# Gate and value of three token chunks in seven products of 64x64 tiles, with the last batch's attention and the weight sums moved ahead of them

## The chip, the core and the metric

The kernel runs on one core of a Trainium2 chip. The metric is the time of one execution on the device in microseconds; the kernel before takes 289.92 us, the median of three runs (289.42 to 290.87). Everything is float32. The engines are named as the profile names them: PE is TensorE's matrix multiply and PEld its weight loads, DVE is VectorE, ACT is ScalarE, POOL is GpSimd, SP is the engine that issues most DMAs. PSUM holds what PE writes, in eight banks of 128 partitions by 512 numbers; SBUF holds everything else.

## What is computed

A polynomial sketch attention over four batches, four heads, 1088 positions of 32 numbers each, and then a gated feed-forward layer over all 4 x 1088 = 4352 tokens of 128 numbers:

```python
# attention, for each batch and head
a, b = S1 @ x, S2 @ x                        # 8 numbers each
phi(x) = outer(a, b)                         # 64 features
kv, z = phi(k).T @ v, phi(k).sum(over positions)
x = (phi(q) @ kv) / (phi(q) @ z + 1e-6)
# then, over x as (4352, 128), with 1536 hidden units
gate = 1 / (1 + exp(-(x @ w_gate)))
val = x @ w_val
out = (gate * val) @ w_out
```

## The kernel before

The four batches of attention write their result, transposed, into one SBUF tile `xT` of 128 partitions (one for each input feature) by 4352 tokens. The feed-forward layer takes the tokens in chunks of 512: chunks 0 to 7, and chunk 8 of 256 tokens. A chunk needs the batches that its tokens lie in: chunk 5 ends in batch 2, chunk 6 takes 192 tokens of batch 2 and begins batch 3, chunk 7 and 8 lie in batch 3.

**A wave** (`w1`, line 556) computes the gate and the value of 128 hidden units for a chunk: four matmuls with all 128 rows of the array, two for each of gate and value, because each is split in two column halves of 64 hidden units (`128*64` in the profile; the two halves run side by side). A float32 matmul is two instructions. ACT takes the sigmoid of the gate (line 564), DVE multiplies it with the value (line 599, for chunk 8 line 592), and the result `g` goes to SBUF. Twelve waves make a chunk; chunk 8 takes two times 128 units in a wave and has six. The PSUM tile of a wave has two banks and there are two such tiles, so wave n+2 can start when DVE has done the product of wave n. Waves are counted from 0; chunk 5 begins with wave 60, chunk 8 with wave 96.

**The output** of chunks 1 to 7 is already computed by a scheme with seven products instead of eight, of pairs of waves (`w2_a`, `w2_b`, line 381). It splits the tokens, the hidden units and the output features in halves; POOL makes the four sums of `g` that it needs (`token_sums`, line 371), the sums of the weights stand ready in `ws`. Each product has 256 columns and is `128*64`. At the end of a chunk ACT and DVE put the result together (lines 486 to 533) and SP stores it (line 393). Chunk 8's output is computed with plain products (`w2_end`, line 451), and its end is the end of the kernel (`store_end`, line 407).

**The order of the work** on PE, DVE, ACT and POOL is that of the program text; nothing reorders it. `slot(group, waves)` puts out one wave after another: it first puts out the DVE product of the wave before, then the output products that are due (`todo`), then the wave. The attention of batches 2 and 3 is set between the waves by a list of wave numbers, `plan`: transposing k and q (lines 662, 673), `begin` (the sketch, and DMAs that spread it through DRAM, line 864), the outer products (line 772), the sums of the features (line 946), `kv_all` (line 912), the products of q's features (line 892), and `parts`, which divides and writes `xT` (lines 1041 to 1304). For batch 3 the list is 48, 49, 52, 54, 57, 58, 59, 60, 62, 63, 65, 67. The k and q of batch 3 are loaded right after the last step but one of batch 2, at wave 41.

Of the kernel before, what the change touches and what calls it, by code (L numbers as in the profile page):

```python
# [8 lines left out]
F32 = mybir.dt.float32  # L9
# [3 lines left out]
ALU = mybir.AluOpType  # L13
ACTF = mybir.ActivationFunctionType
MUL = ALU.mult

P = 128


@with_exitstack  # L20
def kernel(
# [20 lines left out]
    assert DM == H * D == P and D == 32 and R == 8 and S % 32 == 0 and NTOK % 512 == 256  # L42

    T = S // 32

    NJK = 9
    KBASE = [0, 9, 17, 25]
# [5 lines left out]
    ld = ctx.enter_context(tc.tile_pool(name="ld", bufs=1))  # L53
    sbA = ctx.enter_context(tc.tile_pool(name="sbA", bufs=2))
    raw = ctx.enter_context(tc.tile_pool(name="raw", bufs=NJ // 2))
    sbN = ctx.enter_context(tc.tile_pool(name="sbN", bufs=1))
    sbG = ctx.enter_context(tc.tile_pool(name="sbG", bufs=3))

    dram = ctx.enter_context(tc.tile_pool(name="dram", bufs=1, space=bass.MemoryType.DRAM))

    psm = ctx.enter_context(tc.tile_pool(name="psm", bufs=2, space=bass.MemoryType.PSUM))
    pso = ctx.enter_context(tc.tile_pool(name="pso", bufs=1, space=bass.MemoryType.PSUM))
    ps2 = ctx.enter_context(tc.tile_pool(name="ps2", bufs=1, space=bass.MemoryType.PSUM))

    ctx.enter_context(tc.manual_schedule(
            engines={
# [62 lines left out]
    class Short:  # L129
# [31 lines left out]
        def total(self):  # L161
            nc.gpsimd.tensor_tensor(  # L162
                out=self.head, in0=self.head, in1=self.tail.bitcast(I32), op=ALU.add
            )
# [183 lines left out]

    xT = const.tile([P, NTOK], F32, tag="xT")

    moe = {"sum": -1, "ci": 0, "w": 0, "n": 0, "ready": 0, "acc": None, "gate": None, "todo": [], "late": [], "copies": []}

    def fast(ci):
        return 0 < ci < len(tok_chk) - 1 and tok_chk[ci][1] == TCH

    def weight_sums(n0, n1):
        w = w_sb[:, 2].rearrange("p (n f) d -> p f n d", f=2)[:, :, n0:n1]
# [22 lines left out]
    def product(out, lhsT, rhs, start, stop):  # L380
        nc.tensor.matmul(  # L381
            out=out, lhsT=lhsT, rhs=rhs, start=start, stop=stop, skip_group_check=True
        )
# [18 lines left out]

    def store_end(acc):
        b, r = divmod(tok_chk[-1][0], S)
        o_sb = [sbA.tile([P, P], F32, tag="o_sb", name="o_end") for _ in range(2)]
        for u, copy in enumerate((nc.scalar.copy, nc.vector.tensor_copy)):
            copy(out=o_sb[u], in_=acc[u])
        for u, eng in enumerate((nc.scalar, nc.sync)):
            eng.dma_start(
                out=bass.AP(  # L410
                    tensor=out.tensor,
                    offset=out.offset + (b * S + r // 32 + u) * DM,
                    ap=[[T * DM, 32], [2 * DM, 4], [1, DM]],
                ),
                in_=o_sb[u],
            )

    def w2(ci, j0, jn, g):
# [13 lines left out]
        if j0 + jn == NJ:  # L432
# [2 lines left out]
            moe["store"] = lambda: store(  # L435
                ci, lambda g4: o_sb[32 * g4 : 32 * g4 + 32], nc.scalar
            )

    def w2_end(ci, j0, jn, g):
        if j0 == 0:  # L440
            moe["sum"] = ci
            moe["acc"] = [
                pso.tile([P, TCH], F32, tag="acc0", name="moeout0")[:, :DM],
                ps2.tile([P, 2, TCH], F32, tag="two", name="moeout1")[:, 0, :DM],
            ]
        acc = moe["acc"]
        for u in range(2):
            for jj in range(jn):
                j = j0 + jj
                for c in (u * P, u * P + 64):  # L450
                    nc.tensor.matmul(  # L451
                        out=acc[u][c % P : c % P + 64],
                        lhsT=g[:, jj, c : c + 64],
                        rhs=w_sb[:, 2, j, :],
                        start=(j == 0),
                        stop=(j == NJ - 1),
                    )
        if j0 + jn == NJ:
            store_end(acc)


    fst = {}

# [31 lines left out]
    def add(out, in0, in1):  # L495
        nc.vector.tensor_tensor(out=out, in0=in0, in1=in1, op=ALU.add)  # L496
# [44 lines left out]
    def w1():  # L541

        ci = moe["ci"]
        t0, tw = tok_chk[ci]
        jn = TCH // tw
        j0 = moe["w"] * jn
        wv = psm.tile([P, 2, TCH], F32, tag="wave", name="wave")

        tp = tw // 2 if ci == 0 and j0 == 0 else tw
        turn = (moe["w"] // 2) % 2  # L550
        for o in range(0, tw, tp):
            for which in range(2):
                for jj in range(jn):
                    for c in (0,) if ci == 0 else (1 - turn, turn):
                        d = slice(0, P) if ci == 0 else slice(64 * c, 64 * c + 64)
                        nc.tensor.matmul(  # L556
                            out=wv[d, which, jj * tw + o : jj * tw + o + tp],
                            lhsT=w_sb[:, which, j0 + jj, d],
                            rhs=xT[:, t0 + o : t0 + o + tp],
                            start=True,  # L560
                            stop=True,
                        )
        sg = sbG.tile([P, TCH], F32, tag="sg", name="sg")
        nc.scalar.activation(out=sg, in_=wv[:, 0], func=ACTF.Sigmoid)  # L564
        if ci == 0:
            if j0 == 0:
                step("final", 2)
                step("sign", 3, bank="acc1")
            if j0 == 1:
                step("final", 3)  # L570
            if 1 < j0 < NJ - 1:
                narrow_w(j0 + 1, 3)
            if j0 > 0:
                narrow_w(j0 + 2, 1)
                narrow_w(j0 + 2, 2)
            if j0 < 3:
                narrow_w(j0 + 3, 0)
            if j0 > 1:
                narrow_w(j0 + 4, 0)
            if j0 == NJ - 3:  # L580
                weight_sums(0, NJ // 4)
            if j0 == NJ - 1:
                weight_sums(NJ // 4, NJ // 2)
        if moe["w"] % 2 == 0:
            moe["g"] = sbG.tile([P, 2, TCH], F32, tag="g", name="g")
        pair, odd, n = moe["g"], moe["w"] % 2, moe["n"]

        def glu():
            g = pair[:, odd]
            todo = moe["todo"]  # L590
            if jn == 2:
                nc.vector.tensor_tensor(  # L592
                    out=g.rearrange("p (j u s y) -> p j y u s", j=2, u=2, y=4),
                    in0=wv[:, 1].rearrange("p (j y u s) -> p j y u s", j=2, u=2, y=4),
                    in1=sg.rearrange("p (j y u s) -> p j y u s", j=2, u=2, y=4),
                    op=MUL,
                )
            else:
                nc.vector.tensor_tensor(out=g, in0=wv[:, 1], in1=sg, op=MUL)  # L599
            if not fast(ci):  # L600
                lag = 4 if ci else 2
                part = (ci, j0, jn, g.rearrange("p (j t) -> p j t", j=jn))
                todo.append((n + lag, lambda: (w2_end if ci else w2)(*part)))
                return
            if not odd:
                moe["t"] = raw.tile([P, 4, HALF], F32, tag="w_in", name="tsum")
            token_sums(pair, moe["t"], odd)
            if odd:
                part = (ci, j0 // 2, pair, moe["t"])
                todo.append((n + 3, lambda: w2_a(*part)))  # L610
                todo.append((n + 4, lambda: w2_b(*part)))

        moe["gate"] = glu
        moe["w"] += 1
        moe["n"] += 1
        if j0 + jn == NJ:
            moe["ci"] += 1
            moe["w"] = 0
# [6 lines left out]
    def slot(group, waves, behind=None):  # L625

        if group is not None:
            group()
        todo = moe["todo"]
        for _ in range(waves):  # L630
            more = moe["ci"] < len(tok_chk)
            if more and sum(tok_chk[moe["ci"]]) > moe["ready"]:
                break
            glu()
            for _ in range(2 if moe["ci"] >= len(tok_chk) - 1 else 1):
                if moe["late"]:
                    moe["late"].pop(0)()
            while todo and todo[0][0] <= moe["n"]:
                todo.pop(0)[1]()
            if behind is not None:  # L640
                behind()
                behind = None
            if more:
                w1()
            for copy in moe["copies"]:
                copy()
            moe["copies"] = []
            if more:
                continue
            if not todo:  # L650
                break
            else:
                todo.pop(0)[1]()

    kT_of, qT_of = {}, {}

# [688 lines left out]
    slot(None, 1)  # L1345
    slot(lambda: parts(1), 1)
    moe["store"]()

    def until(n):
        slot(None, n - moe["n"])  # L1350

    plan = {2: (27, 29, 30, 31, 32, 34, 36, 37, 38, 39, 41, 43)}
    plan[3] = (48, 49, 52, 54, 57, 58, 59, 60, 62, 63, 65, 67)
    for b in range(2, B):
        at = iter(plan[b])
        until(next(at))
# [22 lines left out]
        load_kq(b + 1)  # L1379
        until(next(at))  # L1380
        slot(lambda: parts(b), 1)
    slot(None, 10**3)


# [28 lines left out]
```

## Time and profile before

| what | us |
| --- | --- |
| median of three runs | 289.92 |
| the profiled execution, span from its first to its last instruction | 288.1 |
| PE busy | 282.6 |
| DVE busy | 170.5 |
| POOL busy | 160.0 |
| ACT busy | 106.6 |
| start of wave 60 (first of chunk 5) in the chain that ended last | 174.26 |
| start of chunk 8's first wave there | 266.68 |
| end of the last matmul | 284.9 |

The span is one execution, taken by the profiler on the core; the 1.8 us between it and the median lie before its first and after its last instruction, or are the difference of one execution from another. In the profile's groups of instructions a row gives the source line, the engine, the operation, the tile written and those read, the shapes and the count, and behind the bar the busy time in us and the mean duration of one in ns. In the timeline a row begins with its start and its length in us; rows of equal instructions that follow each other are merged into one. A matmul's length there is longer than its share of PE, because matmuls are pipelined: the time from one start to the next is what it costs.

### The profile page before, as it was taken

The page shows a single profiled execution, that of the slowest core. Times are in us where ns is not written, and L with a number is a line of the kernel's source. Part 1 is how long each engine was busy: PE and PEld are TensorE (multiplying, and loading weights), DVE is VectorE, ACT ScalarE, POOL GpSimd, SP SyncE. Part 2 cuts the span into 40 slices and gives each one's busy share as a digit, 9 for nine tenths or more (in the row PEclk, how much of TensorE's full clock was granted, in tenths as well). Part 3 has the DMA queues.
Part 4 walks back from the last instruction along what each step waited for, and adds up shares of the span by engine and source line. Part 5 has one row for each costly group of instructions (what it writes and reads, how often), then busy time and mean ns, then how long its engine had stood idle before and what let it go on. Part 6 is the DMA issues. An engine that isn't in the chain of part 4 may idle for free.

```text
span 288.1 us, 5783 instructions
## 1 busy us (share of the span) xinstructions
PE 282.6 (98%) x2260; PEld 135.1 (47%) x2260; DVE 170.5 (59%) x292; ACT 106.6 (37%) x215; POOL 160.0 (56%) x222
## 2 busy tenths in 40 slices
PE   8899999999999999999999999999999999999995
PEld 4454433354444444535444445444444444444685
DVE  6977788945748547668446485767245223522571
ACT  3688833222334322523244222532243224421341
POOL 2666682667466387383565496483564646555200
PEclk9999999999999999999999999999999999999999
DMA  7995441766500385352000683020001000020012
GB/s 220 348 360 124 104 156 43 171 150 157 164 3 2 77 198 166 92 161 32 1 0 12 162 158 123 2 30 9 0 3 23 14 2 0 4 35 1 0 19 40
DMA packets 28891, 24.24 MB, mean 84 GB/s; under 512 B 18560, under 2 KB 24064, under 8 KB 28864
## 3 DMA queue, kind: packets, MB, share of 16 engines
q1 hardware_dynamic: 25888, 22.10, 30.1%
q10 hardware_dynamic: 2976, 1.77, 2.1%
q8 instruction: 18, 0.29, 0.4%
q14 instruction: 9, 0.07, 0.1%
HBM read 20.60 MB, written 3.26 MB: 83 GB/s over the span
## 4 chain that ended last, share of the span: by engine, by line
PE 97%; ACT 1%; POOL 0%; DVE 0%; issue 0%
PE wave L556 61%; PE prod L381 22%; PE moeout L425 4%; PE moeout L451 2%; PE warm L301 2%; PE kvz L912 1%; PE nps L1270 1%; PE kps L693 1%; PE kvz L899 1%; PE cqps L839 1%; PE nps L1102 0%; PE denj L1041 0%; PE nps L1054 0%; PE dps L1083 0%; ACT asb L810 0%; POOL gh L727 0%
## 5 line engine op out<-in xcount | busy, mean ns | idle before, releaser
L556 PE MATMUL wave<-xT,w_sb 128*64 128x512 f32 (+3 forms) x820 | 201.4, 565 | 0.1
L564 ACT ACTIVATE sg<-wave 128x512 f32<-128x512 f32 x102 | 60.9, 597 | 158.3 <-PE wave L556 152.3
L599 DVE TENSOR_TENSOR g<-wave,sg 128x512 f32<-128x512 f32 x96 | 66.1, 688 | 87.9 <-ACT sg L564 86.3
L371 POOL TENSOR_TENSOR tsum<-g,tsum 128x256 f32<-128x256 f32 x84 | 68.6, 817 | 71.0 <-DVE g L599 70.9
L556 PEld LDWEIGHTS wave<-xT,w_sb 128*64 128x64 f32 (+1 forms) x820 | 71.0, 140 | 72.7 <-issue 53.0
L371 POOL TENSOR_TENSOR tsum<-g 128x256 f32<-128x256 f32 x84 | 66.6, 793 | 22.1 <-DVE g L599 21.5
L381 PE MATMUL prod<-tsum,ws 128*64 128x256 f32 x252 | 68.4, 380 | 0.0
L381 PE MATMUL prod<-g,w_sb 128*64 128x256 f32 (+1 forms) x170 | 50.3, 378 | 0.0
L381 PEld LDWEIGHTS prod<-tsum,ws 128*64 128x64 f32 x252 | 34.0, 137 | 13.1 <-issue 9.7
L381 PEld LDWEIGHTS prod<-g,w_sb 128*64 128x64 f32 x170 | 23.0, 137 | 30.1 <-issue 25.8
L381 PE MATMUL prod<-tsum,w_sb 128*64 128x256 f32 x84 | 25.0, 380 | 0.0
L381 PE MATMUL prod<-g,ws 128*64 128x256 f32 x84 | 25.0, 379 | 0.0
L162 POOL TENSOR_TENSOR head<-head,tail 128x384 int32<-128x384 int32 (+1 forms) x13 | 13.2, 1023 | 4.4 <-DVE head L157 4.4
L381 PEld LDWEIGHTS prod<-g,ws 128*64 128x64 f32 x84 | 11.5, 137 | 5.7
L425 PE MATMUL moeout<-g,w_sb 128*128 128x512 f32 (+1 forms) x26 | 12.4, 596 | 0.0
L381 PEld LDWEIGHTS prod<-tsum,w_sb 128*64 128x64 f32 x84 | 11.3, 137 | 1.3 <-issue 1.0
L592 DVE TENSOR_TENSOR g<-wave,sg 128x512 f32<-128x512 f32 x6 | 6.8, 1134 | 6.3 <-ACT sg L564 4.7
L772 DVE TENSOR_TENSOR kp<-kab 128x1152 f32<-128x1152 f32 (+1 forms) x8 | 10.2, 1289 | 0.0
L892 DVE TENSOR_TENSOR qp<-qp,bq 128x1152 f32<-128x1152 f32 (+1 forms) x7 | 10.1, 1444 | 0.0
L496 DVE TENSOR_TENSOR res<-prod,other 128x256 f32<-128x256 f32 x14 | 5.9, 425 | 6.3 <-ACT other L487 4.8
L141 POOL TENSOR_SCALAR head<-cap 128x384 f32<-128x384 f32 (+1 forms) x13 | 6.2, 483 | 4.6 <-ACT cap L140 4.6
L152 ACT ACTIVATE tail<-w_in,two__157 128x384 f32<-128x384 uint32 (+1 forms) x12 | 7.3, 618 | 0.0
(130 smaller groups left out, 197.5 us busy)
## 6 DMA issues: line engine op xcount, KB each, us to landing
qp<-dq SPq DMA_DIRECT2D x7, 576.0 KB
bq<-dq SPq DMA_DIRECT2D x14, 288.0 KB
kq<-in_k_dram SPq DMA_DIRECT2D x3, 544.0 KB
kq<-in_q_dram SPq DMA_DIRECT2D x3, 544.0 KB
w_in<-in_moe_w_out_dram SPq DMA_DIRECT2D x6, 256.0 KB
w_in<-in_moe_w_gate_dram SPq DMA_DIRECT2D x5, 256.0 KB
w_in<-in_moe_w_val_dram SPq DMA_DIRECT2D x5, 256.0 KB
v<-in_v_dram SPq DMA_DIRECT2D x8, 144.0 KB
```

What stands on the lines that cost most here:

```text
L141: nc.gpsimd.tensor_scalar(out=self.head.bitcast(F32), in0=self.cap, scalar1=122880.0, scalar2=2.0**-15, op0=ALU.min, op1=ALU.max,)
L152: nc.scalar.activation(out=self.tail, in_=self.lo, func=ACTF.Identity, bias=two, scale=2.0**-51)
L162: nc.gpsimd.tensor_tensor(out=self.head, in0=self.head, in1=self.tail.bitcast(I32), op=ALU.add)
L371: nc.gpsimd.tensor_tensor(out=t[:, u], in0=in0, in1=in1, op=ALU.subtract)
L381: nc.tensor.matmul(out=out, lhsT=lhsT, rhs=rhs, start=start, stop=stop, skip_group_check=True)
L425: nc.tensor.matmul(out=moe["acc"][d], lhsT=w_sb[:, 2, j, d], rhs=g[:, jj], start=(j == 0), stop=(j == NJ - 1),)
L556: nc.tensor.matmul(out=wv[d, which, jj * tw + o : jj * tw + o + tp], lhsT=w_sb[:, which, j0 + jj, d], rhs=xT[:, t0 + o : t0 + o + tp], sta ...
L564: nc.scalar.activation(out=sg, in_=wv[:, 0], func=ACTF.Sigmoid)
L592: nc.vector.tensor_tensor(out=g.rearrange("p (j u s y) -> p j y u s", j=2, u=2, y=4), in0=wv[:, 1].rearrange("p (j y u s) -> p j y u s", j ...
L599: nc.vector.tensor_tensor(out=g, in0=wv[:, 1], in1=sg, op=MUL)
L772: eng.tensor_tensor(out=KP[b][:, pi, j0:j1].rearrange("p j m (i l) -> p (j m) i l", i=R), in0=bass.AP(tensor=a0.tensor, offset=a0.offset, ...
L892: nc.vector.tensor_tensor(out=q0, in0=q0, in1=half(BQ[b], n), op=MUL)
```

## The change

1. **Gate and value of chunks 5 to 7** leave the waves. A new function `section` works in windows of two times 128 hidden units, six in a chunk, eighteen in all, and computes the gate and the value of a window together with seven products instead of eight, each with 64 of the 128 rows of the array and 64 of its columns (64x64 tiles). The first four products of a window (P1, P2, P5, P3) use one half of the rows (`lead`), the last three (P6, P7, P4) the other (`tail`), and odd windows exchange the halves. The sums that the scheme needs on the side of the gate and value add up in PSUM in three steps: ACT copies the first product from one bank to another (`Aa`) and another to SBUF (`Ac`), DVE adds (`D1`, `D2`), ACT takes the sigmoid (`Sa`, `Sc`), DVE multiplies (`M1`, `M2`), and PE adds its next product to what stands in the bank between these steps.
2. **The output products** of these chunks, and of the last two pairs of chunk 4, which are held back (`HELD = 2`), are each split in an upper and a lower half of the rows as well (`WL`, `WU`), except for the last four windows (`WF`, all rows). The order of all instructions of the section is written out in a string of 698 items, `ORDER`.
3. **The weights' sums** that the scheme needs, `fw`, are made by seven DMAs on ACT's queue and ten additions on DVE with 768 numbers on each partition (64 or 128 partitions), set at waves 24 to 37 (`cross_weights`, called after batch 1's `parts`). **The tokens' sums** are made for each chunk by four DMAs on SP, which copy `xT`'s halves to both row halves, and four subtractions on POOL.
4. **Batch 3's attention** is put at waves 44, 45, 45, 46, 47, 48, 49, 51, 54, 55, 56, 58.
5. Chunk 8's waves and output products are put out by the section as well, between and behind the last windows. At the section's start the PSUM pools of the waves are closed, and six single banks are opened in their place.

```diff
+    SECT, HELD, BUF = 5, 2, 0
+    LOAD_AT, SUM_AT = (19, 19, 20, 20, 22, 22, 23), (24, 25, 25, 30, 30, 31, 32, 34, 34, 37)
...
+    def cross_weights():
...
+            every = slice(0, P)
+            ops = [
+                (every, f[1], v, f[2], ALU.add),
+                (lead, f[2], g, f[0], ALU.add),
+                (lead, f[2], f[2], f[1], ALU.subtract),
+            ]
+            if turn == 0:
+                ops += [(tail, f[2], f[0], f[2], ALU.subtract), (tail, f[0], f[1], f[0], ALU.subtract)]
+            else:
+                ops += [(tail, f[0], f[1], g, ALU.subtract), (tail, f[1], g, v, ALU.subtract)]
...
+        loads = [lambda o=o, i=i: nc.scalar.dma_start(out=o, in_=i) for o, i in loads]
+        for at, many in ((LOAD_AT, loads), (SUM_AT, sums)):
+            for n in at:
+                moe["prep"].append((n, many.pop(0)))
...
@@ in slot(), after each wave
+            while moe["prep"] and moe["prep"][0][0] < moe["n"]:
+                moe["prep"].pop(0)[1]()
...
     moe["store"]()
+    cross_weights()
...
-    plan[3] = (48, 49, 52, 54, 57, 58, 59, 60, 62, 63, 65, 67)
+    plan[3] = (44, 45, 45, 46, 47, 48, 49, 51, 54, 55, 56, 58)
...
-    slot(None, 10**3)
+    def load_y(c):
...
+        for k, src in enumerate((LO, HI)):
+            for dst in (LO, HI):
+                nc.sync.dma_start(out=y[dst, k], in_=xT[src, t0 : t0 + TCH])
...
+    def section():
...
+        early.close()
+        pg = ctx.enter_context(tc.tile_pool(name="pg", bufs=1, space=bass.MemoryType.PSUM))
+        bank = [pg.tile([P, TCH], F32, tag=f"b{x}", name=f"b{x}") for x in range(6)]
+        GA, GC, V = (bank[BUF], bank[4]), (bank[BUF + 1], bank[5]), (bank[2 - BUF], bank[3 - BUF])
...
+        def feature(k, nn, w):
...
+            rows, lhsT, rhs, dst = {
+                "P1": (lead, gate if even else f[:, 0], y[:, 0, :HALF], GA),
+                "P2": (lead, f[:, 0] if even else gate, y[:, 1, :HALF], GA),
+                "P5": (lead, f[:, 1], s[:, 0], GC),
+                "P3": (lead, f[:, 2], y[:, 1, HALF:], GC),
+                "P6": (tail, f[:, 0], s[:, 1], V),
+                "P7": (tail, f[:, 2 if even else 1], s[:, 2], V),
+                "P4": (tail, val if even else f[:, 2], s[:, 3], V),
+            }[k]
+            start = k in ("P1", "P5") and (k, w) not in started
+            for c in range(2):
+                product(
+                    dst[w % 2][half_of(c), nn * HALF : (nn + 1) * HALF],
+                    lhsT[rows, half_of(c)], rhs[rows], start, False,
+                )
...
+        def gated(k, w):
...
+            if k == "Aa":
+                nc.scalar.copy(out=v, in_=ga)
+            elif k == "Ac":
+                nc.scalar.copy(out=s5, in_=gc)
+            elif k == "Sa":
+                nc.scalar.activation(out=sg[:, :, first], in_=two(ga), func=ACTF.Sigmoid)
+            elif k == "Sc":
+                nc.scalar.activation(out=sg[:, :, second], in_=two(gc), func=ACTF.Sigmoid)
+            elif k == "D1":
+                add(gc, v, s5)
+            elif k == "D2":
+                add(c2, v, s5)
+            elif k == "M1":
+                nc.vector.tensor_tensor(out=g[:, :, first], in0=two(v), in1=sg[:, :, first], op=MUL)
+            else:
+                nc.vector.tensor_tensor(out=g[:, :, second], in0=two(c2), in1=sg[:, :, second], op=MUL)
...
+    at = NJ * SECT
+    until(at - 6)
+    load_y(0)
+    for u in range(4):
+        until(at - 4 + u)
+        x_sum(0, u)
+    until(at)
+    glu()
+    if SECT + 1 < len(tok_chk) - 1:
+        load_y(1)
+    for x in moe["late"]:
+        x()
+    section()
```

The written order begins so (`P1:1` is the first product of window 1 for its first 128 units, `P1':1` for its second; the letters are those of the functions above; `Q` are the token sums on POOL, `T` the sums of `load_y`'s tokens, `E` the copies of a finished output bank and `F` its totals, `C`, `Y`, `Z`, `O` are chunk 8):

```
P1:1 P1:0 T2:1 P1':0 WUB:-2.0 P5:1 WLA:-2.1 P5:0 P1':1 Aa:0 P5':0 P5':1 Aa:1 P2':0 P6':0 P2:0 P6:0
Ac:0 P6':1 P2:1 Ac:1 D1:0 P2':1 P6:1 Sa:1 D1:1 P3:0 P7:0 P3':0 P7':0 Sa:0 P7':1 P3':1 D2:0 T0:1 P7:1
P3:1 P1:2 P4':0 Sc:1 D2:1 P1':2 P4:0 Sc:0 P4:1 P1:3 M1:0 P1':3 P4':1 P5':3 P5':2 Aa:2 M1:1 P5:3
```

## Prediction

> **What bounds the kernel now.** I read the page's busy times, then the chain that ended last, then the timeline of single stretches.
>
> ```profile
> PE 282.6 (98%) x2260; PEld 135.1 (47%) x2260; DVE 170.5 (59%) x292; ACT 106.6 (37%) x215; POOL 160.0 (56%) x222
> ...
> PE 97%; ACT 1%; POOL 0%; DVE 0%; issue 0%
> ```
>
> PE is the chain: only less column work on PE, or idle that is put into it, moves the end. The granted clock is 1.000 throughout. From the chain in order of time (start, length, what), a wave, output products, and batch 2's `kv` with the products behind it:
>
> ```profile
> 143.31 1.72 PE wave L556 x8
> 145.03 0.86 PE prod L381 x8
> ...
> 178.56 1.14 PE kvz L912 x72
> 179.81 1.01 PE prod L381 x8
> ```
>
> A wave is 8 instructions of 512 columns in 1.72 us, two abreast: a **round** costs 0.43 us, and for the products' 256 columns 0.86 / 4 = 0.215 us. After a stretch of other tiles the same eight products cost 1.01 + the 0.11 us gap ahead of them instead of 0.86.
>
> The span (288.1) is 1.8 us under the median of the runs; changes are summed in the span and added to 289.92.
>
> **1. Gate and value in 64x64 tiles.** Two waves (256 hidden units) are 8 rounds of 0.43, so 3.43 us. A window for the same units is 7 products x 2 (units) x 2 (column halves) x 2 instructions = 56 of 256 columns. If four run abreast, that is 14 rounds of 0.215 = 3.01. Saved: 0.42 a window, 7.6 us for 18. A check from the other end: from wave 60 (174.26) to the last matmul (284.9) are 110.6 us, of which batch 3's `kv` (1.4), `ndt` (0.2) and `parts` (1.8) go elsewhere, leaving 107.2. The section's PE work is 252 half-row items and 112 half-row output items of one round each (78.3), 14 full-row output items of two rounds (6.0), 24 of chunk 8's gate and value (10.3) and 24 of its output (5.4, from 3.56 us for the last 63): 100.0. Saved so: 7.2. I take **-7.4**.
>
> Do four run abreast? The trace has the case:
>
> ```profile
> 128.84 1.16 PE L1270 MATMUL nps<-qp,nd 64*32 64x512 f32 x32
> ```
>
> 32 instructions on 64-row tiles, 16 of them with 512 columns. Two abreast those 16 alone would take 3.4 us; all 32 took 1.16, upper and lower rows side by side, each half writing its own bank. In the written order upper and lower items alternate (never three running in one half, balance within one item), and neighbours in opposite halves never write one bank. So I price a round at 0.215; the bound above is 0.239, by the first round of `kps`, whose second pass starts 0.266 after the first instead of 0.242.
>
> Weight loads double (56 + 28 per window in 4.5 us). In the timeline:
>
> ```profile
> 241.36 0.38 PE L381 MATMUL prod<-g,w_sb 128*64 128x256 f32 x1
> 241.36 0.14 PEld L381 LDWEIGHTS prod<-g,ws 128*64 128x64 f32 x1
> ...
> 241.58 0.38 PE L381 MATMUL prod<-g,ws 128*64 128x256 f32 x1
> ```
>
> The next product's weights load beside a running matmul of the same 128 rows, and the next start is still 0.215 on: loads cost nothing here, and I take the same for four tiles. [...]
>
> **2. The section's start.** The built program's first product of window 1 waits for DVE's product of wave 59, because the six banks replace the waves' pools as a whole. PE then has nothing else queued. How long that is, a wave in the timeline tells:
>
> ```profile
> 239.43 1.89 PE L556 MATMUL wave<-xT,w_sb 128*64 128x512 f32 x8
> ...
> 241.37 0.60 ACT L564 ACTIVATE sg<-wave 128x512 f32<-128x512 f32 x1 [1.98 <-PE wave L556]
> ...
> 242.00 0.69 DVE L599 TENSOR_TENSOR g<-wave,sg 128x512 f32<-128x512 f32 x1 [1.82 <-ACT sg L564]
> ```
>
> The wave's columns are through at 241.15, where the next product starts (a round before the one shown above); the DVE product ends at 242.69. With 0.05 for the wait: **+1.6** idle. Before, 0.86 of products and the next wave cover this. Everything else on PE is queued behind that wait.
>
> **3. Changes of tile shape.** The end mixes full-row items with halves: five changes beyond the start's, three of them back to full rows. The return after `kv` cost 0.11 + 0.15; into smaller tiles 0.02 (first round 0.080 instead of 0.056). I take 3 x 0.19 + 2 x 0.02 = **+0.6** (0 to 1.3).
>
> **4. Waits within the section.** A step between PE and another engine needs 0.165 (end of a 256-column matmul: 380 ns long, 215 apart) + its instruction + about 0.1. By these groups:
>
> ```profile
> L564 ACT ACTIVATE sg<-wave 128x512 f32<-128x512 f32 x102 | 60.9, 597 | 158.3 <-PE wave L556 152.3 <-DMA dq<-cq 4.0 <-DVE z L946 2.0
> ...
> L599 DVE TENSOR_TENSOR g<-wave,sg 128x512 f32<-128x512 f32 x96 | 66.1, 688 | 87.9 <-ACT sg L564 86.3 <-POOL tsum L371 1.5
> ```
>
> ACT's copies of 512 take 0.60 (its copy `asb` 0.589), DVE's additions 0.69. The trace has none from PSUM to PSUM; I keep 0.6 and 0.69, bounded by 0.55 and by 1.13 (line 592's reordered product). Need: 0.87 after P1, 0.96 after P6 (`D1`) and P7 (`D2`). Room counted in the written order: P1 to P2 at least 6 rounds (1.29), median 9; P6 to P7 and P7 to P4 at least 6 (1.29), median 7 (1.51), but 4 and 5 rounds in windows 0 and 1. So a lone step fits by 0.3 or more, except in windows 0 and 1: **+0.3** there. Queues: a window lasts 21 rounds = 4.5 us; DVE has 4 x 0.69 and 0.55 of totals (3.3), ACT 2.6, POOL 4 x 0.73 to 0.82 and 0.4 (3.3 to 3.7). None is the bound, but two windows share each queue, and an instruction that finds another ahead of it is up to 0.69 late against 0.3 to 0.6 of room. I take one such miss of 0.2 in every fourth window: **+0.9** (0 to 4).
>
> **5. Ahead of the section.** Batch 3's PE work is moved, not changed. Its DVE work lands on busier stretches:
>
> ```profile
> 133.90 0.69 DVE L1304 TENSOR_TENSOR xT<-num,rb 128x512 f32<-128x512 f32 x1
> 134.51 0.22 DVE L1304 TENSOR_TENSOR xT<-nps,rb 128x64 f32<-128x64 f32 x1
> 134.64 0.68 DVE L599 TENSOR_TENSOR g<-wave,sg 128x512 f32<-128x512 f32 x1
> 135.90 0.69 DVE L599 TENSOR_TENSOR g<-wave,sg 128x512 f32<-128x512 f32 x1 [0.58 <-ACT sg L564]
> ```
>
> Transposing k (1.30) now stands ahead of the product at 134.64, wave 43's, already late after batch 2's `parts`. It ends at 136.6 instead of 135.3; wave 45 needs its banks and started at 135.84: +0.75. Its data are there: the load was issued at 124.9, and DMAs are quiet from 132. The feature sum at 51 (2.4 us) ahead of wave 50's product: +0.2. Shorter gaps inside (`begin` to the q product) stay nine waves.
>
> Weight sums: the ten additions (768 numbers; 0.93 by line 772's shape) cost DVE 9.5 us in waves 24 to 37, mostly in its idle time. But all seven loads are issued in a row on ACT after wave 23's sigmoid (78.88), since the wave counter has passed their numbers. Batch 0's four stores on ACT took 2.0, so seven take 3.6: the sigmoid of 81.05 comes at 82.5. The first sum also stands ahead of wave 24's product, waiting for loads (landing 1.6 to 2 us after issue). That product then ends at 84.2 (wave 26: 84.27), and two sums and k's transpose follow: +0.5. SP's loads of `y` queue behind the spreads, needed 20 us later. Sum of this part **+1.4** (0 to 3).
>
> **The sum:** -7.4 + 1.6 + 0.6 + 0.3 + 0.9 + 1.4 = -2.6; 289.92 - 2.6 = **287.3 us**. The tail is unchanged: chunk 7's totals wait for small DMAs, but DVE's last product is needed some 8 us after they begin and takes about 6.
>
> **Rivals.** (a) *The order holds*: steps 4 and 5 cost nothing; -7.4 + 1.6 + 0.6 = -5.2, 284.7. For it: every lone step fits. Against: DVE at 73% with in-order queues. (b) *The front costs more*: DVE's late products pile up (step 5 at 3.5): -0.5, 289.4, no change. For it: wave 43's product is late already. (c) *Slower: DVE's queue.* D1, D2, M1 and M2 of two windows meet in one queue and PE waits for D1 or D2 in each window. After the start, shapes and front 3.5 us of gain are left, so it decides from 0.2 us of waiting a window; at 0.4 (one collision of 0.69 less 0.3 of room) it is +3.7, 293.6. For it: 4 dependent steps a window. Against: 27% idle and a second window in flight. (d) *It doesn't do what it says*: rounds of four cost 0.239, 364 x 0.024 = 8.7 more, 296.0. Against it: `nps`.
>
> **Chances:** forecast (285.6 to 288.4) 0.40, (a) 0.21, (b) 0.21, (c) 0.14, (d) 0.04. Half a per cent (1.45 us) is about what a measurement of this kernel can tell from no change: faster 0.61, within 0.21, slower 0.18. The range reaches to (a) with a little of step 1's spread, 284.2, and over (b) into the lower part of (c), 291.2.
>
> **What would show it.** Step 1: `64*64` matmuls of one column half and row half starting 0.215 apart, four in each 0.215, and PE's time from wave 60's place to the end near 103. Step 2: one PE gap of 1.6 whose releaser is DVE's `g`. Step 4: PE waits for `b` banks from DVE and ACT below 2 us in all. Step 5: PE gaps of 0.75 near 136 and 0.5 near 85. Wrong: rounds over 0.22, DVE waits in every window, or none at all in front.

## The result and the profile after

The changed kernel takes 292.8 us, the median of eight runs (291.67 to 293.26), against 290.45 for the kernel before (eight runs, 289.42 to 292.33): a ratio of 1.0075, with a 95% interval of 1.005 to 1.01. It is slower by three quarters of a per cent, where 287.3 was forecast. The profiled execution has a span of 291.2 against 288.1; by the forecast's sum it should have been 285.5. So 5.7 us have to be found.

First the page of the changed kernel, its busy times and its chain:

```profile
PE 279.6 (96%) x3204; PEld 158.4 (54%) x3204; DVE 212.1 (73%) x342; ACT 119.4 (41%) x231; POOL 178.5 (61%) x234
...
PE 85%; DVE 7%; DMA 3%; issue 2%; ACT 1%; POOL 1%; ACTq 1%; SPq 0%; DVEq 0%
```

PE is busy for 3 us less than before (slow rounds, shown below, are counted in it), and the chain is no longer PE alone: a seventh of it now runs mostly through DVE, DMAs and ACT. Where that happens is told by PE's waits (total us, number of waits, the longest):

```profile
PE wave L630 <- DVE g L665: 2.7, 2, 2.1
PE b L478 <- DVE g L665: 1.4, 1, 1.4
PE moeout L478 <- DVE g L1634: 1.4, 1, 1.4
```

Four holes, then: one of 2.1 and one of 0.57 among the waves, one at the section's start, one near the end. (A hole here is the time since PE's last matmul ended. Between matmul starts it is longer by what the matmul itself lasts; below I give as "idle" the distance of the starts less the last round's share, 0.215 us behind products of 256 columns and 0.43 behind a wave. Where I say "matched", the starts of the same matmuls in two profiled executions are compared.)

**The large hole, 84 us.** The timeline of ACT, DVE and PE around it:

```profile
78.57 5.61 ACTq L446 DMA_DIRECT2D fw<-w_sb  x7
...
84.28 1.08 ACT L638 ACTIVATE sg<-wave 128x512 f32<-128x512 f32 x2 [5.18 <-DMA fw<-w_sb]
84.59 0.96 DVE L441 TENSOR_TENSOR fw<-w_sb,fw 128x768 f32<-128x768 f32 x1 [4.76 <-DMA fw<-w_sb]
...
85.47 0.68 DVE L665 TENSOR_TENSOR g<-wave,sg 128x512 f32<-128x512 f32 x1
...
86.21 3.63 PE L630 MATMUL wave<-xT,w_sb 128*64 128x512 f32 x8 [2.14 <-DVE g L665]
```

The seven issues of the weight loads keep ACT for 5.61 us. The sigmoid of wave 24 (81.05 before) stands behind them and comes at 84.28, together with the next one. DVE's first weight sum stands ahead of that wave's product and waits for its loads until 84.59. PE's starts at 83.68 and 86.21 are 2.52 apart: 2.31 of idle. And the next wave takes 3.63 us instead of 1.89. The table of stretches says why (length, busy time of PE, PEld, DVE, ACT and POOL, then the granted clock, the DMA engines' share and GB/s):

```profile
86.30:89.60 3.30, 3.30 (x8) 0.88 (x10) 3.23 (x5) 0.00 (x0) 1.74 (x2) 0.50 0.01 2
```

The granted clock is 0.50 there; rounds are 0.855 apart instead of 0.43, four of them, 1.7 us more.

**The end.** Chunk 7's crossing copies (`xb`, DMAs that bring a half of the finished output bank `e` to the other half of the partitions, where DVE's totals need it), and what waits for them:

```profile
274.30 3.76 SPq L490 DMA_DIRECT2D out_dram<-o_sb  x8
...
275.02 0.58 ACT L1593 COPY e<-prod 128x512 f32<-128x512 f32 x1 [3.79 <-PE prod L478]
...
278.16 0.47 SPq L1595 DMA_DIRECT2D xb<-e  x1
...
280.85 0.42 DVE L570 TENSOR_TENSOR r<-e,xb 128x256 f32<-128x256 f32 x1 [6.57 <-DMA xb<-e]
...
281.65 1.05 DVE L1634 TENSOR_TENSOR g<-b,sg 128x512 f32<-128x512 f32 x1
...
282.76 0.44 PE L478 MATMUL moeout<-w_sb,g 128*64 128x128 f32 x4 [1.37 <-DVE g L1634]
```

The source of the first copy is there at 275.6, but SP is issuing the eight stores of chunk 6 until 278.06. The second of the two copies, issued at 278.67, lands 2.05 later, near 280.7, chunk 7's first total has held DVE until then, and chunk 8's product is queued behind it. PE needed that product from 281.3.

### The profile page after: what moved, and what is told of

It is laid out like the page before. It is cut to its first block, busy times and chain, and to the rows that moved or that the text cites. A ratio compares the mean times of both kernels' runs of the same rounds, so it can differ in the third digit from the quotient of the medians.

```text
span 291.2 us, 7846 instructions
## 1 busy us (share of the span) xinstructions
PE 279.6 (96%) x3204; PEld 158.4 (54%) x3204; DVE 212.1 (73%) x342; ACT 119.4 (41%) x231; POOL 178.5 (61%) x234
## 4 chain that ended last, share of the span: by engine, by line
PE 85%; DVE 7%; DMA 3%; issue 2%; ACT 1%; POOL 1%; ACTq 1%; SPq 0%; DVEq 0%
PE wave L630 32%; PE b L478 22%; PE prod L478 20%; PE moeout L522 4%; DVE rb L1356 1%; DVE xT L1367 1%; DMA fw<-w_sb 1%; PE kvz L975 1%; DVE g L665 1%; PE nps L1333 1%; PE kps L756 1%; PE moeout L478 1%; DMA s_in<-in_S_dram 1%; DVE kT L725 1%; DMA xb<-e 1%
## 5 line engine op out<-in xcount | busy, mean ns | idle before, releaser
L630 PE MATMUL wave<-xT,w_sb 128*64 128x512 f32 (+2 forms) x436 | 120.5, 598 | 2.8 <-DVE g L665 2.7
L478 PE MATMUL prod<-tsum,ws 64*64 64x256 f32 (+1 forms) x348 | 82.8, 379 | 0.0
L630 PEld LDWEIGHTS wave<-xT,w_sb 128*64 128x64 f32 (+1 forms) x436 | 41.4, 144 | 49.4 <-issue 35.5
L478 PE MATMUL b<-yt,fw 64*64 64x256 f32 x792 | 64.1, 377 | 1.4 <-DVE g L665 1.4
L665 DVE TENSOR_TENSOR g<-wave,sg 128x512 f32<-128x512 f32 x60 | 41.0, 683 | 25.1 <-ACT sg L638 25.1
L478 PE MATMUL prod<-g,w_sb 64*64 64x256 f32 (+2 forms) x234 | 55.2, 377 | 0.0
L478 PEld LDWEIGHTS b<-yt,fw 64*64 64x64 f32 x792 | 42.3, 133 | 12.3 <-DVE g L665 2.3
L478 PEld LDWEIGHTS prod<-tsum,ws 64*64 64x64 f32 (+1 forms) x348 | 42.8, 135 | 8.4 <-issue 4.3
L478 PE MATMUL prod<-tsum,w_sb 64*64 64x256 f32 (+1 forms) x116 | 33.3, 379 | 0.0
L478 PE MATMUL prod<-g,ws 64*64 64x256 f32 (+1 forms) x116 | 33.3, 378 | 0.0
## 6 DMA issues: line engine op xcount, KB each, us to landing
bq<-dq SPq DMA_DIRECT2D x14, 288.0 KB
```

Source lines behind the costliest of these rows:

```text
L478: nc.tensor.matmul(out=out, lhsT=lhsT, rhs=rhs, start=start, stop=stop, skip_group_check=True)
L630: nc.tensor.matmul(out=wv[d, which, jj * tw + o : jj * tw + o + tp], lhsT=w_sb[:, which, j0 + jj, d], rhs=xT[:, t0 + o : t0 + o + tp], sta ...
```

## The experiments

The theory after this reading: (A) the weight loads cost about 4 us, by two blockers side by side (ACT's issues hold the sigmoid; DVE's sum waits for the landing) and the halved clock behind the hole; (B) chunk 6's store in SP's queue costs 1.4 at the end; (C) the section itself does what was forecast. Main rivals: ACT's queue alone costs it; DVE's added work costs it wherever it stands. Where a time is compared with the kernel before, that ran on the same chip beside it (medians 289.77, 289.9 and 289.85 in the three groups).

**1. Loads on SP's queue**

```diff
-        loads = [lambda o=o, i=i: nc.scalar.dma_start(out=o, in_=i) for o, i in loads]
+        loads = [lambda o=o, i=i: nc.sync.dma_start(out=o, in_=i) for o, i in loads]
```

> The seven loads of the weights' halves are issued by SP, which is idle from 70 to 96 us, instead of ACT; nothing else changes. Theory (two blockers side by side: ACT's queue holds the sigmoid of wave 24 until 84.28, and DVE's first weight sum, which stands ahead of wave 24's product, waits for the loads to land until 84.59): the sigmoid comes at 81.05 again, but the sum still ends near 85.5 and the product near 86.2, so PE's gap stays near 2.3 us, the half clock behind it too, and the span stays at 291 (290.7 to 291.3). Rival (ACT's queue alone costs it): the gap is gone, span 287.0.

Measured: 289.18, ratio to before 0.9976 (0.996 to 0.9991), span 287.2. Against both of my numbers the rival's came out, but the edit did more than I thought. The loads' own row (shortest, median, longest issue in ns; first and last start) and, from DVE's timeline, the first sum:

```profile
L446 SPq DMA_DIRECT2D fw<-w_sb x7: 613/699/979, 42.6 to 47.2; - x7
```

```profile
80.37 0.95 DVE L441 TENSOR_TENSOR fw<-w_sb,fw 128x768 f32<-128x768 f32 x1
```

SP's queue waits for data, not for a wave's place in the program, and the weights are there early: the loads are issued at 42.6, not at 78. So nobody waits for landings either, and both blockers are gone at once. The run shows that the loads cost all of it (no hole at 84; matched with the changed kernel, PE's starts are 0.3 us later ahead of that place and 3.8 earlier behind it, so 4.1 are gained there); it does not tell the two blockers apart.

**2. The first three sums later, loads on ACT**

```diff
-    ... (24, 25, 25, 30, 30, 31, 32, 34, 34, 37)
+    ... (26, 28, 28, 30, 30, 31, 32, 34, 34, 37)
```

> The first three weight sums on DVE are moved from waves 24, 25, 25 to 26, 28, 28; the loads stay on ACT. Theory (two blockers): ACT still holds the sigmoid until 84.28, the product ends near 85.6 instead of 86.15, so PE idles 1.7 instead of 2.3 us; as the gap of 1.8 at the section's start had no halved clock behind it, the rounds of the next wave come 0.43 apart again and not 0.86: span 291.2 - 0.6 - 1.7 = 288.9; if the clock is halved all the same, 290.6. Rival (the sum's wait alone costs it): span 287.0. Rival (ACT's queue alone): 291.2.

Measured: 292.52, ratio 1.0082 (1.0061 to 1.0103), span 289.8. DVE's products and PE's next wave:

```profile
85.06 1.29 DVE L665 TENSOR_TENSOR g<-wave,sg 128x512 f32<-128x512 f32 x2 [5.19 <-ACT sg L638]
...
85.81 1.94 PE L630 MATMUL wave<-xT,w_sb 128*64 128x512 f32 x8 [1.71 <-DVE g L665]
```

With the sum out of the way ACT alone makes 1.87 us of idle (starts 83.72 and 85.81), and the next wave runs at full clock, as expected. What I had not expected is behind it: the moved sums meet the transposes of batch 2's k and q, and two new holes appear (starts 95.54 to 96.16 and 99.85 to 101.12; 0.41 and 1.05 idle). Matched with the changed kernel, 2.1 us are gained at the first hole and 1.5 are given back at these two.

**3. Both**

> Both: loads issued by SP, first three sums at waves 26, 28, 28. Theory: wave 24's sigmoid near 81.05, its product near 81.7 to 82.5, no PE gap near 84 and a full clock there: span 291.2 - 2.3 - 1.7 = 287.2 to 287.4, time about 288.9 against 292.8 for the changed kernel. Rival (DVE's added work makes products late wherever the sums stand): 1 us or more of new gaps between 82 and 95, span 288.5 or more.

Measured: 291.21, ratio 1.0046 (1.003 to 1.0063), span 290.2. My number failed and the rival's held: there is no hole at 84, but holes of 0.81 and 1.05 idle at 95 and 100. Loads early and sums at 24 and 25 (the first run) are 2 us better than loads early and sums at 26 and 28. The sums are cheap at their old places once their data are there.

**4. Loads on SP, meant to be late**

```diff
+        nc.sync.dma_start(out=fw[0][:64, 1, 0, :32], in_=xT[:64, 2 * S - 32 : 2 * S])
```

> The seven loads are issued by SP as in loads_on_sync, but behind a small copy of batch 1's last 32 tokens, which exist at 77.9 us: so they are issued when ACT issued them (near 78.3) and not at 42.6, and ACT is free. Theory (two blockers side by side: ACT's issues hold the sigmoid, and DVE's first sum, ahead of wave 24's product, waits for the landing): the sigmoid of wave 24 is on time near 81, the sum waits until 84 to 84.6, the product ends near 85.8, PE idles 1.9 to 2.3 us, span 289.2 to 291. Rival (ACT's issues alone cost it, the landing is in time when nothing else is in the way): no gap, span 287.2 as with the loads at 42.6.

Measured: 289.89, ratio 0.9988 (0.9967 to 1.0008), span 288.4. It tells nothing on the question: the loads were issued at 42.8 again, ahead of the small copy at 78.7, because they don't depend on it. It showed something else, 0.55 of idle in the section (starts 235.57 to 236.34), which comes back in 5, 10 and 11.

**5. The same with a dependence on each load**

```diff
+        for k in (0, 2):
+            nc.sync.dma_start(
+                out=fw[0][:, k, 1:3, :8], in_=xT[:, S : S + 16].rearrange("p (n d) -> p n d", n=2)
+            )
```

> The seven loads are issued by SP, but each has to wait for two small copies of batch 1's first tokens into the same tile, which exist at 76.4 us: so SP issues the loads from about 78.5 to 84, when ACT issued them, and ACT is free. Theory (two blockers side by side: ACT's issues hold the sigmoid of wave 24, and DVE's first sum, ahead of wave 24's product, waits for the fourth load to land): the sigmoid is on time near 81, the sum waits to 84.5 or longer, PE idles 2 to 3.5 us, span 289.5 to 292. Rival (ACT's issues alone cost it): no gap, span 287.2 as with the loads at 42.6.

Measured: 291.89 (290.76 to 295.56), ratio 1.0066 (1.0039 to 1.0093), span 292.4 (this execution lost 2 us in its first 20). From its timeline, SP's issues, the sigmoid of wave 24, the first sum and wave 26:

```profile
80.62 5.62 SPq L450 DMA_DIRECT2D fw<-w_sb  x7
...
83.17 0.60 ACT L642 ACTIVATE sg<-wave 128x512 f32<-128x512 f32 x1 [1.57 <-PE wave L634]
...
86.56 0.96 DVE L441 TENSOR_TENSOR fw<-w_sb,fw 128x768 f32<-128x768 f32 x1 [4.24 <-DMA fw<-w_sb]
...
88.18 1.94 PE L634 MATMUL wave<-xT,w_sb 128*64 128x512 f32 x8 [1.62 <-DVE g L669]
```

ACT is free, the sigmoid of wave 24 is on time after its matmuls, and still PE idles 1.8 us (starts 86.18 and 88.18): the sum waits until 86.56 for loads issued from 80.62 on. So either blocker alone leaves a hole: 1.8 us here, 1.9 in experiment 2, 2.3 with both. Counted from PE's last start ahead of the hole, the loads were issued 0.45 us earlier here than in the changed kernel (80.62 to 86.18 against 78.57 to 83.68); issued no earlier, the landing alone would come to about 2.2, an estimate. So taking only the issues away from ACT would save next to nothing. The rival "ACT alone" falls.

**6. The kernel before with the weight loads and sums alone**: `cross_weights` and its call are put into the kernel before; nothing uses the sums.

> The kernel before with the seven loads on ACT and the ten weight sums on DVE as in the change, whose results nothing uses. Theory: the same stall as in the changed kernel, 2.3 us of PE idle near 84, followed in about half of the executions by 3.4 us at half the clock (1.7 more): span 290.4 or 292.1, time 292.2 to 293.9; so this part alone is more than the whole difference between the two kernels. Rival (the stall needs the section's pools or the moved attention): the predicted 0.5, span 288.6.

Measured: 293.97, ratio 1.0131 (1.0097 to 1.0165), span 292.5.

The same hole at the same place (starts 83.78 and 86.31, DVE's product the releaser). Behind it the granted clock is 1.00 until 87.4 and 0.50 from there to 90.8 (0.67 in the mean of 86.30 to 89.60). This part alone costs 4.1 us in the median, more than the changed kernel loses in all: the section earns, and the preparation spends more. The other three executions have a mean clock of 0.998 or more and still spans of 291.4 to 291.9, over 3 us above 288.1, of which the hole is 2.3; what makes up the rest in them no trace shows. In experiment 8, 0.7 us are lost behind the same hole at full clock.

**7. The kernel before with batch 3's attention moved alone**

> The kernel before with batch 3's attention at waves 44 to 58 as in the change, and nothing else. Theory (the move costs only wave 45's wait behind k's transpose): one gap of 0.95 between two starts after batch 2's division, span 288.1 + 0.5 = 288.6. Rival (batch 3's work collides with more of the work of waves 46 to 58): further gaps, 1 us or more, span 289.6 or more.

Measured: 290.85, ratio 1.003 (1.001 to 1.0049), span 289.2. The one hole is wave 45's (starts 135.82 to 136.77; 0.74 idle, not the 0.52 I had written). Matched with the kernel before, PE's starts are 0.2 us later from the first 9 us on and 1.1 later behind batch 3's attention, so the move costs 0.9, nearly all of it in this hole. The median is 1.0 above the kernel before. The forecast had 0.95 for the two parts of the move.

**8. Chunk 6's store behind chunk 7's crossing copies**

```diff
- ... WFA:14.0 F6:1 WFA:17.0 ...   C1:5 EB:2 C0:5 ...
+ ... WFA:14.0 WFA:17.0 ...        C1:5 EB:2 F6:1 C0:5 ...
```

> The transpose and store of chunk 6 (eight DMA issues on SP, 3.76 us) are put behind the issue of chunk 7's crossing copies. Theory (the crossing copies stood behind the store in SP's queue, DVE waited for them until 280.85, and chunk 8's last but one product stood behind DVE's wait): the copies are issued near 275.6 instead of 278.2, PE's gap of 1.43 at 281 goes, span 289.8. Rival (the second pair of copies lands too late anyway, since its source is there only at 278.1): the gap stays at 0.8 or more, span 290.6 or more.

Measured: 290.88, ratio 1.0029 (1.0008 to 1.0051), span 288.1. From its timeline, the first copy, chunk 7's first total and chunk 8's product:

```profile
274.70 0.47 SPq L1595 DMA_DIRECT2D xb<-e  x1
...
277.38 0.43 DVE L570 TENSOR_TENSOR r<-e,xb 128x256 f32<-128x256 f32 x1 [4.58 <-DMA xb<-e]
...
278.19 1.10 DVE L1634 TENSOR_TENSOR g<-b,sg 128x512 f32<-128x512 f32 x1
```

The first copy is issued 0.55 us behind its source, with four of the stores still ahead of it, the product comes 3.5 us earlier (1.5 of them from further ahead), and the hole is gone; matched with the changed kernel, the last matmuls gain 1.6 there. The span fell by 1.5 more than that, which is not this edit. The hole at 84 is the same (starts 83.89 and 86.41), but in this execution the granted clock behind it (86.4 to 89.8) was 1.00. The four rounds there take 1.7 us less, and 0.7 of that is lost again by 93 us, so 1.0 is left. Another 0.7 is a wait near 224 us that this execution does not have (step 4 below), and its first 9 us took 0.2 more.

**9. k's and q's transposes one wave later** (with the loads on SP)

```diff
-    plan[3] = (44, 45, 45, 46, 47, 48, 49, 51, 54, 55, 56, 58)
+    plan[3] = (45, 46, 46, 46, 47, 48, 49, 51, 54, 55, 56, 58)
```

> loads_on_sync with batch 3's transposes of k and q one wave later (45, 46, 46 instead of 44, 45, 45). Theory (k's transpose of 1.3 us ahead of wave 43's product holds wave 45): the gap of 0.95 between two starts at 136 goes (0.52 idle), span 287.2 - 0.5 = 286.7. Rival (the same work only delays a later product): a gap of 0.3 to 0.6 appears in waves 46 to 48, span 287.2.

Measured: 289.21, ratio 0.9969 (0.9943 to 0.9994), span 287.1. Wave 45's hole is gone (its starts come 0.74 earlier, matched against run 1), and a smaller one follows a wave later (starts 138.78 to 139.35); 0.38 is kept. In the median, 289.21 against run 1's 289.18, that can't be seen.

**10. The first held pair ahead of the section** (with the loads on SP)

```diff
-P1:1 P1:0 T2:1 P1':0 WUB:-2.0 P5:1 WLA:-2.1 P5:0 ...
+WFA:-2.0 WFB:-2.0 WFA:-2.1 P1:1 P1:0 T2:1 P1':0 P5:1 P5:0 ...
```

and the other four items of that pair taken out further on.

> loads_on_sync with the six half-row output items of the first held pair of waves taken out of windows 0 to 3 and put, as three full-row items (12 instructions, 4 x 0.43 / 4 each: 1.29 us), ahead of the section's first product. Theory (PE is idle there for 1.79 us because everything stands behind the wait for wave 59's product): the hole between matmul starts shrinks from 2.0 to 0.7, windows 0 to 3 have 1.3 us less work between their steps and lose 0 to 0.5 of it in waits: span 287.2 - 1.3 + 0.3 = 286.2. Rival (the output items were the cover of the steps in windows 0 to 3): new waits of 1 us or more before D1, D2 or the copies, span 287.0 or more.

Measured: 289.09, ratio 0.9976 (0.9956 to 0.9996), span 286.8. The hole shrank from 2.0 to 0.50 between starts. The first gate product still begins 2.01 after wave 59's last start, since it waits for that wave's product; from it to the last matmul the section takes 103.0 instead of 103.6. So of 1.29 that were moved, 0.54 are gained in the end. Matched with run 1, the gain had grown to 1.28 by 229 us, and 0.74 of it went into one wait at 233.8, the one that experiment 4 had shown without this edit. Neither of my two numbers: the cover in windows 0 to 3 was not needed, but a wait came later, and whether this edit has a part in it is open.

**11. Four edits together** (1, 8, 9 and 10)

> The four edits together: loads on SP, chunk 6's store behind chunk 7's crossing copies, k's and q's transposes one wave later, the first held pair ahead of the section. If the four losses are separate, they add: 287.2 - 1.4 (the gap at the end) - 0.5 - 1.0 = 284.3 in the span, about 286.2 in time, 1.2% below the kernel before. Rival (one loss only hides another, as when the section's start moves and DVE's queue at its start is later): 285.5 or more in the span.

Measured: 286.96, ratio 0.9912 (0.9879 to 0.9945). The profiled execution is its slowest (span 288.0, with 2.2 us lost in the first 14 and 1.2 near 74); the other five have spans of 284.4 to 285.2, below the rival's 285.5. The losses are separate and add, but for 0.6 (median 284.9, forecast 284.3). One hole in the section is left, of 0.58; DVE there:

```profile
236.30 0.50 DVE L570 TENSOR_TENSOR r<-e,xb 128x256 f32<-128x256 f32 x1 [1.02 <-DMA xb<-e]
...
236.73 0.69 DVE L570 TENSOR_TENSOR b<-b,s 128x512 f32<-128x512 f32 x1
```

It is the end's mechanism in small: chunk 5's first total waits for its crossing copy, and window 13's addition, for which PE waits, is queued behind it.

**12. A fifth edit**: that total (`F0:0`) is put next to the second (`F1:0`), a window later.

> The four edits, and chunk 5's first total on DVE, which waited for its crossing copies to land (1.02 us) with window 13's first addition queued behind it, stands next to its second total, a window later. Theory: PE's gap of 0.79 between two starts at 236.7 goes (0.58), span of most executions 284.9 - 0.5 = 284.4, time 286.5. Rival (the later total only delays another addition): a gap of the same size elsewhere, 284.9.

Measured: 286.86 (286.08 to 288.59), ratio 0.9897 (0.9863 to 0.9931), span 284.2. The hole is gone from this execution, where the addition no longer stands behind that total. That alone shows little: the hole stands in the profiles of experiments 4, 5, 10 and 11, and not in those of the changed kernel or of 1, 2, 3, 8 and 9, all with the total at its old place. And matched with run 11, the 0.6 us gained there are preceded by 0.5 lost at 219, where PE waits for a token sum of POOL that took 1.18 us instead of 0.74. Its page:

```profile
PE 278.4 (98%) x3192; PEld 163.4 (57%) x3192; DVE 212.9 (75%) x342; ACT 119.4 (42%) x231; POOL 179.9 (63%) x234
...
PE 92%; DVE 5%; issue 1%; ACT 1%; POOL 0%; DVEq 0%
```

This version is about 1.0% faster than the kernel before. Against run 11 the median moves by 0.1; whether the fifth edit is worth anything is open.

## Why the forecast was wrong, step by step

**Step 1, right.** Four 64x64 tiles run abreast, a round every 0.216 us, with the weight loads beside them. A round and the begin of the next, in the timeline of PE alone (`x2` is two instructions):

```profile
241.36 0.38 PE L478 MATMUL prod<-g,ws 64*64 64x256 f32 x1
241.37 0.38 PE L478 MATMUL prod<-tsum,ws 64*64 64x256 f32 x1
241.37 0.38 PE L478 MATMUL b<-yt,w_sb 64*64 64x256 f32 x2
241.57 0.38 PE L478 MATMUL prod<-g,ws 64*64 64x256 f32 x1
```

Four starts, and 0.21 later the next. From the section's first matmul to its last are 104.0 us, with the hole at the end in them, and PE is busy for 102.6 of them, where near 103 was named, and PEld for 77.3. The starts are four in nearly every round: from 188.6 to 224.0 there are 652 where 35.4 / 0.216 x 4 = 656 fit, and from 225.6 to 260.4 there are 642 where 644 fit. The first 350 rounds took 76.9 us instead of 75.3; 0.9 of that are the two waits of step 4, and the rest is rounds of 0.216 instead of 0.215, a few places left empty, and the first rounds.

**Step 2, right**: forecast 1.6, and one hole of 1.58 idle (starts 181.77 to 183.77, less a wave's round of 0.43), with the releaser named in the timeline of DVE and PE:

```profile
182.40 1.32 DVE L665 TENSOR_TENSOR g<-wave,sg 128x512 f32<-128x512 f32 x2
...
183.77 0.43 PE L478 MATMUL b<-yt,fw 64*64 64x256 f32 x2 [1.41 <-DVE g L665]
```

**Step 3, right**: the five changes of shape show 0.09 + 0.05 each, 0.7 in all (forecast 0.6).

**Step 4, near in size, only in part as told**: two waits, 0.9 us in all instead of 1.2. The first is 0.2, for one of DVE's additions (starts 187.51 to 187.92). The second is for POOL (starts 224.25 to 224.66, with half of the places empty from 224.03 on): PE's next product reads a token sum that POOL ends at 224.60, after 1.17 us. In experiment 8 the same sum takes 0.72, PE does not wait, and the matmuls behind it come 0.65 earlier, matched. DVE's queue has room; the rival (c) did not happen as told. Its mechanism, an addition behind another instruction in DVE's queue, is seen in experiments 4, 5, 10 and 11, but the instruction in front is one that waits for a DMA, chunk 5's first total (rows of 11 above).

**Step 5, the step that failed.** Its first part was right: k's transpose ahead of wave 43's product held wave 45 by 0.73 (starts 139.85 to 140.79; forecast 0.75), as the timeline shows; there is no hole at wave 52.

```profile
138.86 1.30 DVE L725 STREAM_TRANSPOSE kT<-kq 128x1088 f32<-128x1088 f32 x1
...
140.79 1.94 PE L630 MATMUL wave<-xT,w_sb 128*64 128x512 f32 x8 [0.57 <-DVE g L665]
```

Its weight loads are the term that failed: they were put at +0.5 and cost 4.1 (experiment 1, matched; 2.3 of idle and 1.7 of slow rounds). The mechanism was named, the sigmoid behind seven issues and the sum ahead of the product; three sizes were wrong. An issue was taken from batch 0's stores (2.0 / 4 = 0.5); these take 0.62 to 0.95, the last ones longest, with the gaps between them 5.61 instead of 3.6, so the sigmoid came at 84.28 and not 82.5. A landing was taken as 1.6 to 2 us behind its issue, from single transfers; with seven of 192 KB in flight the fourth landed 3.9 behind (80.63 to 84.5). And the cost of a hole was taken as its length: behind this one the clock was halved, 0.994 in the mean of the execution, in six of eight. The bound of 3 for the whole step was built on the same prices, so it was no bound.

**"The tail is unchanged", wrong.** I counted DVE's work against the time and left out SP's queue. Chunk 6's eight stores stand there ahead of the crossing copies: +1.4, at a term that the forecast put at nothing.

**The sum**, against the forecast span: +3.6 for the loads, +1.4 for the end, +0.4 in the section's first 350 rounds (76.9 us, where 75.3 and 1.2 of waits were named), +0.3 in the rest of the section, +0.2 because -7.4 was taken where the check from the other end gave -7.2, -0.1 at waves 45 and 52, and -0.4 in the first 70 us, which differ by some tenths from one execution to another; that is 5.4 of 5.7, and 0.3 lies in small places. The sign came from none of the rivals: (b) has the right place but, at 3.5 for the whole step, too small a price.

## What to carry to other kernels

When a change puts DMAs on a compute engine's queue, price the issues from transfers of the same shape and number, and then ask separately who is behind the issues and who waits for the landing: if both lead to the same consumer, undoing one shows almost nothing (here 1.8 and 1.9 us of idle were left of 2.3). SP's queue, which has no compute work, issued these loads as soon as their data allowed, at 42.6 instead of 78.6, 36 us earlier and without a hole. And before a tail is called unchanged, list what already stands in the queue of each transfer that it waits for.

## What was not expected of the hardware

- **The halved clock behind a hole.** In the changed kernel the clock was 0.994 in the mean of six of eight executions and 0.999 or more in two, which were about 1.1 us faster; with the same hole of 2.3 us, five of ten executions of experiment 8 were at 0.994 or below, and one of four of experiment 6. Where the hole was 1.8 to 1.9 (experiments 2 and 5) it was one of fourteen. The slow stretch lasts 3.41 us (86.28 to 89.70 by the trace's clock record).
- **Where the halved clock begins.** In the changed kernel it begins at 86.28, with PE's first wave behind the hole (start 86.21). In experiment 6 PE had run at full clock for 1.1 us behind the hole before the clock fell. It also falls behind the last matmul: in the changed kernel's trace 3.3 us behind its end (287.78 to 291.08), in that of the kernel before 4.9 (284.88 to 289.82). What decides in a given execution whether the clock falls, and where, was not tried, and no run here shows it.
- **DVE and POOL take longer beside each other.** Of the changed kernel's ten weight sums six took 0.94 to 0.97 us and four 1.37 to 1.39; the long ones are those that began while one of POOL's token sums had about 0.55 us left to run. POOL's token sums that began beside a weight sum took 1.33 to 1.45 instead of 0.73. So a sum placed beside POOL's work can cost more than its own length. No run here separates the cause.
